# Filter diagonals from unnormalised taps, built as chunk 0 lands; transposes over three PSUM tiles; first group evacuated first

## The chip, the core and the metric

The kernel runs on one core of a Trainium2 chip. The metric is device time in microseconds of one execution, the median over several executions. The engines of the core are named as the profile names them: PE (matrix multiply; PEld is its weight loading), DVE (VectorE), ACT (ScalarE), POOL (GpSimd), and SP, which here only issues DMAs.

## What is computed

Two stages, the second fed by the first. `x` has 8 batches of 4096 tokens of 192 channels, in float32.

```python
w = exp(weight - max(weight)); w = w / sum(w)        # 8 heads x 7 taps
out[b, s, h, g] = sum_k w[h, k] * x_pad[b, s + k, h, g]   # causal, 6 zeros in front
h = out.reshape(32768, 192) @ w_in                   # 192 -> 2048
g = h * sigmoid(beta * h)                            # beta: one number per hidden column
y = g @ w_out                                        # 2048 -> 192
```

The first stage is a softmax over seven taps and a causal convolution along the tokens, the same for the 24 channels of a head. The kernel computes `silu(beta * h) @ (w_out / beta)`, which is the same as `g @ w_out`.

## The kernel before

**Tiling.** A chunk is 512 tokens of two batches, `b` and `b + 4`. The 192 channels are held as three groups of 64, and the two batches lie in the two halves of the 128 partitions, so a group is a tile of 128 partitions by 512 tokens. There are 32 chunks. For each, channels must lie on partitions, so `x` is cast to bf16 and transposed; the convolution gives `ct` (three groups); 16 hidden columns of 128 (index `u` or `fc`) are computed by `hidden`: six matmuls of 64 rows each, the two batches in the two halves of the array, then a Silu on ACT into `g`; and `Job` objects multiply `g` with `w_out_s` into the tiles `pa` and `pb`, some pairs of matmuls after each hidden column.

**Later chunks** are transposed by DMA and convolved on DVE (`tap`, L338 and L340). Their work is put between the hidden columns of the chunks before.

**Chunk 0** cannot wait for that. Its tokens land in two DMAs of 256 tokens; four blocks of 128 tokens are cast on DVE (`cast_rows`, L226) into `x0b`, transposed on PE (`transposes`, L233) and evacuated into `xt0` (L302), by ACT for blocks 0, 1 and 3 and by DVE for block 2. Groups 0 and 1 are then convolved on PE: `diag_tap` (L287) multiplies the shifted tokens with a diagonal matrix per tap, and seven of them add up in PSUM; ACT evacuates the sums (L330). Of group 2, taps 5 and 6 go this way and taps 0 to 4 run on DVE (L338, L340), and L352 adds the two.

**The taps.** `weight` is spread over the partitions by a small matmul (L244); DVE takes the maximum (L249), ACT the exponential and its sum `total` (L250), DVE the reciprocal (L252) and the product `cw` (L253), the normalised taps. `diags(k0, k1)` (L260) makes the diagonal matrices of taps `k0` to `k1 - 1` out of `cw`: taps 0 and 1 after the second cast, the others after block 2's evacuation.

**Chunk 1** is transposed on PE too (`second`); group 0 is convolved with the same diagonals in `conv1`, between hidden columns 4 to 6 of chunk 0, and evacuated by DVE (`conv1_evac`, L403); groups 1 and 2 are convolved on DVE by `conv_ops`, taken from `queue`.

**Weights.** The first 256 columns of `w_in` come by SP's queue in float32 and are cast by ACT (L332). The other columns come by eight DMAs that POOL issues (L211) and that cast on the way; two DMAs for each piece of columns, rows 0 to 63 and 64 to 127. In front of them stands a copy of one number (`hold`, L274) that makes POOL wait for `cw`. `w_out` comes by SP in four pieces and is divided by `beta` in `scale_w_out` (L314), pieces 0 and 1 on POOL and 2 and 3 on DVE. `beta` itself is transposed on PE (L308) and copied by ACT (L309); its reciprocal is L354.

**Order.** The schedule is written out by hand: each engine runs its instructions in the order in which the code emits them, and the framework adds the semaphore waits. `first_work` lists what is emitted after which hidden column of chunk 0; `None` there means the next entry of `queue`. `fill` (L223) emits matmuls of zeros between the early steps. PSUM is held in three pools: `psum_h` with two tiles and `psum_a` and `psum_b` with one each, every tile two banks large.

Of the kernel before, what the change touches and what calls it, by code (L numbers as in the profile page):

```python
# [9 lines left out]
FP32 = mybir.dt.float32  # L10
FP32R = mybir.dt.float32r
BF16 = mybir.dt.bfloat16
AF = mybir.ActivationFunctionType
ALU = mybir.AluOpType
# [3 lines left out]
def kernel(  # L18
# [17 lines left out]
    nc = tc.nc  # L36

    B, S, D = x.shape
    H, K = weight.shape
# [3 lines left out]
    NG = D // DG  # L43
    HP = group // NG
    TOK = 512
    NF = F // 128
    PAD = K - 1
    HALO = 16
    BLK = 128
# [12 lines left out]
    setup = ctx.enter_context(tc.tile_pool(name="setup", bufs=1))  # L62
# [18 lines left out]
    def in_a():  # L81
        return psum_a.tile([128, 2, TOK], FP32, name="pa")

    def in_b():
        return psum_b.tile([128, 2, TOK], FP32, name="pb")
# [85 lines left out]
    for i in range(NW - 1):  # L171
# [10 lines left out]
    xt0 = setup.tile([128, NG, HALO + TOK], FP32R)  # L182
# [6 lines left out]
        out=sel,  # L189
# [8 lines left out]
        out=sel,  # L198
# [10 lines left out]
    def load_w_in(c0, c1):  # L209
        for r in range(2):  # L210
            nc.gpsimd.dma_start(  # L211
                out=w_in_s[r * DG : (r + 1) * DG, :, c0:c1], in_=w_in_v[:, :, c0:c1]
            )
# [6 lines left out]
    def fill(n, cols=TOK):  # L220
        zc = zeros.unsqueeze(1).to_broadcast((128, cols // 128, 128))
        for _ in range(n):
            nc.tensor.matmul(pf[:, 0, 0:cols], zeros, zc, start=True, stop=True)  # L223

    def cast_rows(copy, xb, x, b):
        copy(  # L226
            xb[:, b].rearrange("q c h p -> q h c p"),
            x[:, b // 2, :, b % 2].rearrange("q h (p c) -> q h c p", c=NG),
        )

    def transposes(pt, xb, b):
        for c in range(NG):
            nc.tensor.transpose(  # L233
                pt[:, c, :], xb[:, b, c].rearrange("q h p -> q (h p)"), ident_b
            )

    def tokens(xt, b):
        t = HALO + (b // 2) * 2 * BLK
        return xt[:, :, t : t + 2 * BLK].rearrange("p c (q b) -> p c b q", b=2)[:, :, b % 2]


    fill(3)
    pw = in_a()[:, 0, 0:K]
    nc.tensor.matmul(pw, sel.rearrange("i h p -> i (h p)"), w8, start=True, stop=True)  # L244
    fill(5)
    nmax = setup.tile([128, 1], FP32)
    total = setup.tile([128, 1], FP32)
    cw = consts.tile([128, K], FP32)
    nc.vector.reduce_max(nmax, pw, axis=mybir.AxisListType.X, negate=True)  # L249
    nc.scalar.activation(cw, pw, AF.Exp, bias=nmax, accum_out=total)  # L250
    nc.scalar.activation(warm, warm, AF.Silu)
    nc.vector.reciprocal(total, total)  # L252
    nc.vector.tensor_scalar_mul(cw, cw, total)  # L253

    beta = consts.tile([128, NF], FP32)
    beta_r = setup.tile([128, NF], FP32)
    diag = setup.tile([128, K, 128], FP32R)

    def diags(k0, k1):
        nc.vector.tensor_tensor(  # L260
            diag[:, k0:k1],
            ident.unsqueeze(1).to_broadcast((128, k1 - k0, 128)),
            cw[:, k0:k1].unsqueeze(2).to_broadcast((128, k1 - k0, 128)),
            ALU.mult,
        )

    for b in range(NB):
        cast_rows(nc.vector.tensor_copy, x0b, x0, b)
        if b == 1:
            diags(0, 2)  # L270


    hold = setup.tile([1, 1], FP32)
    nc.gpsimd.tensor_copy(hold, cw[0:1, 0:1])  # L274
    load_w_in(F0, FW)
    for i in range(1, NW):
        load_w_in(i * FW, (i + 1) * FW)
# [2 lines left out]
    cts = {}  # L280
# [4 lines left out]
    def diag_tap(k, xt, pv, rows=slice(0, 128), k0=0):  # L285
        o = HALO - PAD + k
        nc.tensor.matmul(  # L287
            pv,
            diag[rows, k, :],
            xt[rows, o : o + TOK],  # L290
            start=(k == k0),
            stop=(k == K - 1),
        )

    pts = [
        pool.tile([128, 2, 2 * TOK], BF16, name=name)
        for pool, name in ((psum_b, "pb"), (psum_h, "ph"))
    ]
    for b in range(NB):
        pt = pts[b % 2][:, b // 2, 0 : NG * BLK].rearrange("p (c q) -> p c q", c=NG)  # L300
        transposes(pt, x0b, b)
        (nc.vector.tensor_copy if b == 2 else nc.scalar.copy)(tokens(xt0, b), pt)  # L302
        if b % 2:
            fill(1, 384 if b > 1 else 128)
    diags(2, 4)
    diags(4, K)
    pb = in_a()[:, 0, 0:NF]
    nc.tensor.transpose(pb, beta_q, ident[0:NF, 0:NF])  # L308
    nc.scalar.copy(beta, pb)  # L309
    fill(1, 128)  # L310

    def scale_w_out(i):
        fcs = slice(i * NQ, (i + 1) * NQ)
        (nc.vector if i > 1 else nc.gpsimd).tensor_tensor(  # L314
            w_out_s[:, fcs, :],
            w_out_raw[:, fcs, :],
            beta_r[:, fcs].unsqueeze(2).to_broadcast((128, NQ, D)),
            ALU.mult,
        )
# [3 lines left out]
    for c in range(NG - 1):  # L323
        pv = in_b() if c else psum_h.tile([128, 2, TOK], FP32, name="ph")
        for k in range(K):
            diag_tap(k, xt0[:, c], pv[:, 0, :])
        if c == 0:
            for b in range(2):
                cast_rows(nc.scalar.copy, x1b, x1, b)
        nc.scalar.copy(cts[0][:, c, :], pv[:, 0, :])  # L330
        if c == 0:
            nc.scalar.copy(w_in_s[:, :, 0:F0], w_in_raw)  # L332
    cast_rows(nc.scalar.copy, x1b, x1, 2)

    def tap(dst, src, k):
        scalar = cw[:, k : k + 1]
        if k == 0:
            nc.vector.tensor_scalar_mul(dst, src, scalar)  # L338
        else:
            nc.vector.scalar_tensor_tensor(  # L340
                out=dst, in0=src, scalar=scalar, in1=dst, op0=ALU.mult, op1=ALU.add
            )

    K_V = 5
    pv = in_a()[:, 0, :]
    for k in range(K_V, K):
        diag_tap(k, xt0[:, NG - 1], pv, k0=K_V)
    dst = cts[0][:, NG - 1, :]
    for k in range(K_V):
        o = HALO - PAD + k  # L350
        tap(dst, xt0[:, NG - 1, o : o + TOK].bitcast(FP32), k)
    nc.vector.tensor_tensor(dst, pv, dst, ALU.add)  # L352
    cast_rows(nc.vector.tensor_copy, x1b, x1, 3)
    nc.vector.reciprocal(beta_r, beta)  # L354
    scale_w_out(0)
    scale_w_out(1)


    def second():
# [39 lines left out]
    def conv1_evac():  # L399
        pv = conv1_ps[0]  # L400
        for r in range(2):
            rows = slice(r * DG, (r + 1) * DG)
            nc.vector.tensor_copy(cts[1][rows, 0, :], pv[rows, r, :])  # L403

    def conv_ops(s, c0):
        def op(k):
# [115 lines left out]
    def rows_of(ch):  # L522
# [3 lines left out]


    first_work = {
        4: [None, None],
        5: [None],  # L530
        6: [conv1_evac, lambda: scale_w_out(2), None],
        7: [None, lambda: rows_of(2)],
        8: [lambda: scale_w_out(3), None],
# [75 lines left out]
```

## Time and profile before

| what | value |
|---|---|
| median of 4 runs | 690.13 us (690.09 to 690.46) |
| profiled execution: its time | 690.46 us |
| profiled execution: its span | 688.7 us |
| PE busy | 683.1 us, 99% |
| ACT busy | 578.8 us, 84% |
| DVE busy | 524.6 us, 76% |
| POOL busy | 10.8 us, 2% |
| granted clock of PE | 1.000 |

The span runs from the first to the last instruction; the execution's own time is 1.8 us more. Times in the profile are microseconds from the start of the span. A row of the profile names the engine, the line of the kernel, the operation and the tiles as `out<-in`, then shapes as partitions by elements, a count, and in brackets the idle time before it and what ended that. The chain of waits is followed back from the last instruction: at each step to what released it, or to the instruction before it on its engine. Instructions of one engine are pipelined, so that one can start up to about 0.1 us before the end of the one before it.

### The profile page before, as it was taken

What the parts mean: (1) busy time and instruction counts of PE and PEld (TensorE: products, weight loads), DVE (VectorE), ACT (ScalarE), POOL (GpSimd) and SP (SyncE); (2) the same over time, 40 slices, a digit from 0 to 9 for tenths busy, and PEclk for the clock granted to TensorE, in tenths of its full rate; (3) what the DMA queues carried; (4) which work ended last, traced back from release to release, by engine and by line L of the source; (5) the groups of instructions that cost most, each with busy time, mean ns of one, the idle gap of its engine ahead of it and who ended that gap; (6) DMA issues with size and microseconds to landing.
All of it is one profiled execution on the core that took longest, in us unless ns stands there. A gap on an engine that the chain in (4) does not pass through costs nothing.

```text
span 688.7 us, 24344 instructions
## 1 busy us (share of the span) xinstructions
PE 683.1 (99%) x11312; PEld 522.2 (76%) x11312; DVE 524.6 (76%) x467; ACT 578.8 (84%) x530; POOL 10.8 (2%) x20
## 2 busy tenths in 40 slices
PE   8999999999999999999999999999999999999998
PEld 4777777777777777777777777777777777777777
DVE  7889877788777797777797777887777977777712
ACT  7988888888888888888888888888888888888893
POOL 5100000000000000000000000000000000000000
PEclk9999999999999999999999999999999999999999
DMA  9744333244332343332344432443323433322111
GB/s 228 188 104 117 105 100 88 60 116 116 93 106 69 85 116 108 101 100 55 104 117 105 93 88 66 116 117 93 105 54 99 117 106 98 97 62 59 49 36 59
DMA packets 121861, 67.06 MB, mean 97 GB/s; under 512 B 53264, under 2 KB 121760, under 8 KB 121760
## 3 DMA queue, kind: packets, MB, share of 16 engines
q1 hardware_dynamic: 120048, 64.12, 34.7%
q0 software_dynamic: 1664, 1.38, 1.2%
q8 instruction: 88, 1.44, 1.0%
q14 instruction: 13, 0.11, 0.1%
q10 hardware_dynamic: 48, 0.01, 0.0%
HBM read 29.89 MB, written 25.17 MB: 80 GB/s over the span
## 4 chain that ended last, share of the span: by engine, by line
PE 98%; DVE 1%; ACT 0%; issue 0%; DVEq 0%; ACTq 0%
PE ph L424 48%; PE pa L457 25%; PE pb L457 24%; PE ph L223 1%; DVE ct L340 0%; PE pb L287 0%; ACT g L432 0%; PE pb L233 0%; DVE ct L352 0%; DVE diag L260 0%; DVE xt L302 0%; PE pa L244 0%; ACT xt L302 0%; DVE ct L338 0%; ACT osb L473 0%
## 5 line engine op out<-in xcount | busy, mean ns | idle before, releaser
L432 ACT ACTIVATE g<-ph,beta 128x1024 bf16<-128x1024 f32 x512 | 569.7, 1115 | 94.9 <-PE ph L424 90.2
L457 PEld LDWEIGHTS <-g 64*128 64x128 bf16 x8160 | 371.0, 94 | 102.2 <-issue 0.2
L424 PE MATMUL ph<-ct,w_in_s 64*128 64x512 bf16 x3072 | 425.2, 376 | 1.0 <-ACT g L432 0.9
L340 DVE SCALAR_TENSOR_TENSOR ct<-xt,cw,ct 128x1536 bf16<-128x1536 bf16 (+2 forms) x190 | 338.0, 1779 | 2.5
L457 PE MATMUL pa<-w_out_s,g 64*128 64x192 bf16 x4112 | 245.3, 243 | 0.0
L457 PE MATMUL pb<-w_out_s,g 64*128 64x192 bf16 (+1 forms) x4048 | 230.4, 243 | 0.0
L424 PEld LDWEIGHTS <-w_in_s 64*128 64x128 bf16 x3072 | 160.0, 94 | 54.7 <-DMA w_in_s<-in_moe_w_in_dram 1.1
L475 DVE TENSOR_REDUCE osb<-pa 128x384 f32<-128x768 f32 x64 | 61.3, 958 | 122.5 <-PE pa L457 121.4
L475 DVE TENSOR_REDUCE osb<-pb 128x384 f32<-128x768 f32 x63 | 60.3, 958 | 29.0 <-PE pb L457 29.0
L106 DVE CAST xb<-xf 128x768 bf16<-128x768 f32 x60 | 40.5, 677 | 0.0
L338 DVE TENSOR_SCALAR ct<-xt,cw 128x1536 bf16<-128x1536 bf16 (+2 forms) x32 | 31.2, 976 | 0.0
L473 ACT COPY osb<-pb 128x192 f32<-128x192 f32 x1 | 0.3, 319 | 7.2 <-PE pb L457 7.2
L223 PE MATMUL ph<-zeros 128*128 128x512 bf16 (+2 forms) x11 | 4.6, 535 | 1.1 <-DVE warm L180 1.1
L211 POOL DMA_DIRECT2D w_in_s<-in_moe_w_in_dram x8 | 5.3, 672 | 0.0
L287 PE MATMUL pb<-xt,diag 64*128 64x512 f32 (+1 forms) x21 | 5.2, 443 | 0.0
L121 DVE COPY xt<-xt 128x18 bf16<-128x18 bf16 x27 | 4.4, 163 | 0.0
L314 POOL TENSOR_TENSOR w_out_s<-w_out_raw,beta_r 128x768 bf16<-128x768 f32 x2 | 3.9, 1964 | 5.4 <-DVE beta_r L354 3.5
L287 PEld LDWEIGHTS pb<-xt,diag 64*128 64x128 f32 (+1 forms) x21 | 3.2, 187 | 1.1 <-issue 0.4
L223 PEld LDWEIGHTS <-zeros 128*128 128x128 bf16 x11 | 1.2, 126 | 2.2 <-issue 1.1
L181 ACT ACT_TABLE_LOAD x1 | 1.3, 1283 | 1.8 <-issue 1.8
L226 ACT CAST x1b<-x 128x384 bf16<-128x384 f32 x3 | 2.0, 718 | 0.0
L233 PEld LDWEIGHTS <-x0b 128*128 128x128 bf16 x12 | 1.2, 129 | 1.0 <-issue 0.5
(55 smaller groups left out, 28.5 us busy)
## 6 DMA issues: line engine op xcount, KB each, us to landing
out_dram<-osb SPq DMA_DIRECT2D x127, 192.0 KB, 2.2
xf<-in_x_dram SPq DMA_DIRECT2D x60, 384.0 KB, 4.4
xt<-xb SPq DMA_TRANSPOSE x120, 2.8
x<-in_x_dram SPq DMA_DIRECT2D x4, 384.0 KB, 4.8
w_out_raw<-in_moe_w_out_dram SPq DMA_DIRECT2D x4, 384.0 KB, 12.7
w_in_s<-in_moe_w_in_dram POOLq DMA_DIRECT2D x6, 192.0 KB, 11.5
w_in_raw<-in_moe_w_in_dram SPq DMA_DIRECT2D x2, 192.0 KB, 6.8
w_in_s<-in_moe_w_in_dram POOLq DMA_DIRECT2D x2, 96.0 KB, 8.4
```

The costliest lines, as they stand in the source:

```text
L106: nc.vector.tensor_copy(xbs[ch][:, :, :, h, :], xfs[ch][:, h].rearrange("q b (p c) -> q b c p", c=NG),)
L121: nc.vector.tensor_copy(dst, last[:, :, HALO + TOK - PAD :])
L211: nc.gpsimd.dma_start(out=w_in_s[r * DG : (r + 1) * DG, :, c0:c1], in_=w_in_v[:, :, c0:c1])
L223: nc.tensor.matmul(pf[:, 0, 0:cols], zeros, zc, start=True, stop=True)
L287: nc.tensor.matmul(pv, diag[rows, k, :], xt[rows, o : o + TOK], start=(k == k0), stop=(k == K - 1),)
L314: (nc.vector if i > 1 else nc.gpsimd).tensor_tensor(w_out_s[:, fcs, :], w_out_raw[:, fcs, :], beta_r[:, fcs].unsqueeze(2).to_broadcast((12 ...
L338: nc.vector.tensor_scalar_mul(dst, src, scalar)
L340: nc.vector.scalar_tensor_tensor(out=dst, in0=src, scalar=scalar, in1=dst, op0=ALU.mult, op1=ALU.add)
L424: nc.tensor.matmul(ph[:, h, :], w_in_s[rows, j, fc * 128 : (fc + 1) * 128], cts[s][rows, j, :], start=(j == 0), stop=(j == NG - 1),)
L432: nc.scalar.activation(gs[s][:, fc], ph, AF.Silu, scale=beta[:, fc : fc + 1])
L457: nc.tensor.matmul(self.po[:, r, b * D : (b + 1) * D], g[rows, fc, self.h, q * BLK : (q + 1) * BLK], w_out_s[rows, fc, :], start=(self.don ...
L475: nc.vector.tensor_reduce(dst, self.po[:, :, 0 : nb * D].rearrange("p r n -> p n r"), axis=mybir.AxisListType.X, op=ALU.add,)
```

## The change

The diagonals are made from `eu`, the exponentials before division by their sum, and the division is applied where the sums leave PSUM, by a factor `rn` per partition: ACT's two evacuations multiply by `rn`, the last sum of group 2 becomes a multiply and add, and chunk 1's evacuation multiplies too. `rn` and `cw` (still used by the taps on DVE) are made after block 2's evacuation.

Taps 0 to 3 of the diagonals are now built before the first cast, the other three after the second cast; POOL's `hold` reads the diagonals and so waits for the first four.

The four transposed blocks go to three tiles in place of two: block 2 to the second bank of the tile that held the taps' product, block 3 to the second bank of `pb`. Blocks 2 and 3 are evacuated in two instructions each, group 0 first and groups 1 and 2 after it. The transposed `beta` goes to a free bank of the second `ph` tile. Piece 1 of `w_out` is scaled on DVE, emitted after hidden column 4 and between the first and the second tap of chunk 1.

```diff
-    pw = in_a()[:, 0, 0:K]
+    pc = in_a()
+    pw = pc[:, 0, 0:K]
...
+    rn = setup.tile([128, 1], FP32)
     cw = consts.tile([128, K], FP32)
+    eu = setup.tile([128, K], FP32)
     nc.vector.reduce_max(nmax, pw, axis=mybir.AxisListType.X, negate=True)
-    nc.scalar.activation(cw, pw, AF.Exp, bias=nmax, accum_out=total)
+    nc.scalar.activation(eu, pw, AF.Exp, bias=nmax, accum_out=total)
     nc.scalar.activation(warm, warm, AF.Silu)
-    nc.vector.reciprocal(total, total)
-    nc.vector.tensor_scalar_mul(cw, cw, total)
...
-            cw[:, k0:k1].unsqueeze(2).to_broadcast((128, k1 - k0, 128)),
+            eu[:, k0:k1].unsqueeze(2).to_broadcast((128, k1 - k0, 128)),
...
+    diags(0, 4)
     for b in range(NB):
         cast_rows(nc.vector.tensor_copy, x0b, x0, b)
         if b == 1:
-            diags(0, 2)
+            diags(4, K)
...
-    nc.gpsimd.tensor_copy(hold, cw[0:1, 0:1])
+    nc.gpsimd.tensor_copy(hold, diag[0:1, 0, 0:1].bitcast(FP32))
...
+    banks = [pts[0][:, 0], pts[1][:, 0], pc[:, 1].bitcast(BF16), pts[0][:, 1]]
     for b in range(NB):
-        pt = pts[b % 2][:, b // 2, 0 : NG * BLK].rearrange("p (c q) -> p c q", c=NG)
+        pt = banks[b][:, 0 : NG * BLK].rearrange("p (c q) -> p c q", c=NG)
         transposes(pt, x0b, b)
-        (nc.vector.tensor_copy if b == 2 else nc.scalar.copy)(tokens(xt0, b), pt)
+        copy = nc.vector.tensor_copy if b == 2 else nc.scalar.copy
+        for cs in (slice(0, 1), slice(1, NG)) if b > 1 else (slice(0, NG),):
+            copy(tokens(xt0, b)[:, cs], pt[:, cs])
         if b % 2:
             fill(1, 384 if b > 1 else 128)
-    diags(2, 4)
-    diags(4, K)
-    pb = in_a()[:, 0, 0:NF]
+    pb = pts[1][:, 1, 0 : 2 * NF].bitcast(FP32)
     nc.tensor.transpose(pb, beta_q, ident[0:NF, 0:NF])
     nc.scalar.copy(beta, pb)
     fill(1, 128)
+    nc.vector.reciprocal(rn, total)
+    nc.vector.tensor_scalar_mul(cw, eu, rn)
 
     def scale_w_out(i):
-        (nc.vector if i > 1 else nc.gpsimd).tensor_tensor(
+        (nc.vector if i else nc.gpsimd).tensor_tensor(
...
-        nc.scalar.copy(cts[0][:, c, :], pv[:, 0, :])
+        nc.scalar.mul(cts[0][:, c, :], pv[:, 0, :], rn)
...
-    nc.vector.tensor_tensor(dst, pv, dst, ALU.add)
+    nc.vector.scalar_tensor_tensor(
+        out=dst, in0=pv, scalar=rn, in1=dst, op0=ALU.mult, op1=ALU.add
+    )
...
-    scale_w_out(1)
...
-            nc.vector.tensor_copy(cts[1][rows, 0, :], pv[rows, r, :])
+            nc.vector.tensor_scalar_mul(cts[1][rows, 0, :], pv[rows, r, :], rn[rows])
...
     first_work = {
-        4: [None, None],
+        4: [None, lambda: scale_w_out(1), None],
```

## The prediction

> **What bounds the kernel now.** I read the page first, for the engine that is never free; then the chain of waits in the first 17 us, where all the edits lie; then the order of time around 16 us, and the DMA queues, for what ends the waits there.
>
> The page, parts 1 and 4 (busy time by engine; the chain that ended last):
>
> ```profile
> PE 683.1 (99%) x11312; PEld 522.2 (76%) x11312; DVE 524.6 (76%) x467; ACT 578.8 (84%) x530; POOL 10.8 (2%) x20
> ...
> PE 98%; DVE 1%; ACT 0%; issue 0%; DVEq 0%; ACTq 0%
> ```
>
> PE is the bound once chunk 0 runs. A start-up edit can only move the moment from which PE is dense, so I ask what sets that. The chain of waits, us 7 to 17:
>
> ```profile
> 7.59 0.55 DVE diag L260
> 8.14 0.47 DVE ct L338
> 8.63 0.77 DVE ct L340
> ...
> 11.85 0.70 DVE ct L352
> 12.55 0.04 issue
> 12.60 0.41 PE ph L424 x2
> ...
> 13.09 2.13 ACT g L432 x2
> 15.21 0.04 issue
> 15.26 0.82 PE ph L424 x6
> 16.08 0.47 PE pb L287 x2
> 16.55 0.57 PE ph L424 x2
> ```
>
> Up to 12.55 the chain is VectorE: the diagonals, then the five taps and the sum of chunk 0's third group. But the step at 16.55 hides a wait, because one half of the array was busy. In order of time, us 16 to 19:
>
> ```profile
> 16.36 0.09 PEld L424 LDWEIGHTS <-w_in_s 64*128 64x128 bf16 x1
> 16.37 1.19 PE L424 MATMUL ph<-ct,w_in_s 64*128 64x512 bf16 x6
> 16.49 2.46 POOL L314 TENSOR_TENSOR w_out_s<-w_out_raw,beta_r 128x768 bf16<-128x768 f32 x1 [1.91 <-DMA w_out_raw<-in_moe_w_out_dram]
> 16.73 0.33 PEld L424 LDWEIGHTS <-w_in_s 64*128 64x128 bf16 x5 [0.28 <-DMA w_in_s<-in_moe_w_in_dram]
> ```
>
> This is hidden column 4 of chunk 0. The weights of rows 0 to 63 are there and load at 16.36; those of rows 64 to 127 (the fourth DMA that POOL issues) are not, and load at 16.73, the moment they land (16.69 by issue 6.51 plus 10.2 to landing, rounded). From there PE has no gap above 0.15 us. So the landing of a weight DMA, and not the VectorE chain, starts the dense stretch. What starts that DMA, POOL in order of time:
>
> ```profile
> 4.17 0.17 POOL L274 COPY hold<-cw 1x1 f32<-1x1 f32 x1 [1.94 <-DVE cw L253]
> 4.29 5.32 POOL L211 DMA_DIRECT2D w_in_s<-in_moe_w_in_dram  x8
> ```
>
> POOL issues the eight weight DMAs behind a copy that waits for `cw`. Last the queues, first us 9 to 10, then 10 to 17; before 9 the view has no packet of q0 at all:
>
> ```profile
> q0 software_dynamic: 27, 0.01, 10.0%
> ...
> q0 software_dynamic: 1082, 0.85, 75.1%
> q1 hardware_dynamic: 1086, 0.82, 45.5%
> ```
>
> The weights' queue q0 starts past 9 and then shares full engines with q1 until about 20.
>
> **The change part by part.** The sum is against the profiled execution (span 688.7, its time 690.46, 0.33 above the median 690.13); the difference is carried to the median.
>
> *Diagonals from `eu`, early.* VectorE loses the reciprocal and multiply at 3.67 to 4.10 and builds four diagonals there. Rows by form: 256 elements 421 ns, 384 elements 554 ns, so 133 ns per 128, and 512 elements about 687 ns: 3.67 to 4.36. Chunk 0's first rows land at 4.30 and the casts start at 4.32; instructions overlap by 0.09, so the first cast is at most 0.04 late. The other three diagonals (554 ns for 427) push casts 2 and 3 from 5.35 to about 5.44. In return 0.89 us of diagonals leaves the chain at 7.25.
>
> *The POOL hold.* It now waits for the first diagonals: 4.36 for 4.10, so hold and all eight weight issues move by **+0.26**. Behind it on POOL stand those DMAs and the first `w_out` scaling, which waits for 12.7 anyway. How much of 0.26 reaches the landing is unknown: nothing if q0's start near 9.4 is set by something else, all of it if set by the issue. From 10 to 17 both queues stay loaded, so a late q0 has no idle engine to catch up on; I take 0.26 and keep 0. An earlier landing is not excluded: VectorE's work beside the issues changes, and the first issue took 913 ns against 627, so I allow −0.29.
>
> The Trainium skill speaks against the whole shift: "DMA: Bandwidth & Descriptors", section "Latency and other measured facts", puts the first byte of a software-generated DMA about 1 us after its issue. The first issue ends at 5.20 and q0's first packets come after 9, so the trace does not agree. If the page were right, something other than the issue would hold q0 back and could absorb the shift: the sum would be 690.13 by the page, 690.39 by the rows.
>
> *Transposes in three tiles, split evacuations.* Block 2 no longer waits for ScalarE's evacuation (6.15): its transposes start near 6.0 for 6.20, and VectorE's copy at 6.55 for 6.78. The 559 ns copy becomes 128 + 256 elements, at 133 ns per 128 about 293 + 426 less 0.09 overlap: 0.63, done 7.18. ScalarE's block 3 likewise ends near 7.35 for 7.47. One more instruction costs 0.07 to 0.16 (smallest rows 98 to 164 ns) on each engine, inside these figures. The convolution matmuls start on the first group, at about 7.1 for 7.52; they are not the chain, VectorE is.
>
> *Reciprocal and `cw` moved here.* 164 + 230 ns and a 35 ns gap, after the copy: 7.09 to 7.52; with the 0.105 gap of a two-semaphore wait the first tap starts at 7.62 for 8.05. Taps unchanged (3.69 to the end of the last): 11.31.
>
> *`rn` in the evacuations.* The sum at L352 (692 ns) becomes a scalar_tensor_tensor; 752 ns is that operation's row: 11.42 to 12.17 for 12.54, **−0.37**. ScalarE's two evacuations cost 583 as CAST; by ACTIVATE rows (1114 ns for 1024, 202 for one element) up to 658. The first has 0.7 us of idle time beside it, the second ends by 11.75, before the 12.17 that PE needs. VectorE's two at L403 (683, 695) cost at most 752: +0.13, against 0.29 of slack (last tap of chunk 1 ends 30.05, PE needs it at 30.38).
>
> *`w_out` scaling 1 from POOL to VectorE.* 0.96 us (the L314 row on VectorE), behind a wait for a DMA that lands at 16.43. Queued behind it: two taps of chunk 1, then the evacuation at 20.50, which waits for PE 0.47. The second of those taps took 2.37 us for 1.28 while POOL scaled; I take 1.28 back. So 16.47, 17.43, 18.7, 20.0: still before 20.50. Off the path; if that cover is gone it costs 1 us per us.
>
> *`beta`'s transpose* goes to a free half of another tile; nothing waits for it before 12.
>
> *Sum.* The 0.37 travels to column 0 (12.22 for 12.60). Column 2 meets its own late weights: 13.71 + 0.26 gives 14.02 for 14.25, so 0.23 is left. Column 4's first half starts near 16.04 for 16.37, and then its second half waits for 16.69 + 0.26 = 16.95, starting 16.99 for 16.73. The gain ends in that wait, and the shift remains: **+0.26 us, 690.39**.
>
> **The rivals.**
> *The issue does not set the landing (0): 690.13.* For: q0 starts 4 us after the first issue. Against: the DMA engines were not full between 6 and 8 us (84.5% busy, 181 GB/s against 328 after 9), so a q0 that was ready would have been served there.
> *Weights are no gate: faster.* The median is 0.33 below the profiled run, about the 0.37 between the two halves of column 4; perhaps in other executions the weights land earlier and PE sets 16.37. Then 16.04 for 16.37: −0.33, 689.80. It decides if the weights land 0.65 us or more earlier than in this profile.
> *VectorE waits for `w_out`: slower.* The scaling sits ahead of chunk 1's taps. It has 20.50 + 0.26 − 20.0 = 0.77, and 0.29 at chunk 1's start: 1.06 in all. It decides if that DMA lands after 17.5. It took 11.6 us to land; with the slowest of its line, 13.7, it costs 2.1 − 1.06 = 1.04 more: 691.43. Against: it is ahead of q0 in time, and q0 starts later now.
> *The change does not do what it says:* the order of instructions shows that it does; only its worth is open.
>
> **How the numbers follow.** Forecast 0.58, no shift 0.17, faster 0.17, `w_out` 0.05, anything else 0.03. The predicted time is the forecast's, 690.39; its own range is 690.20 to 690.60 (a shift of 0.26 give or take 0.2, since runs of one kernel differ by 0.37 here). The range of 8 in 10 takes in the shift of nothing, the earlier landing (690.13 − 0.29 = 689.84) and the faster rival with 0.15 beyond it, and above 0.2 of a late `w_out`: 689.65 to 690.80. All three main cases lie within 0.2% (1.38 us, about what a measurement of this kernel can tell from no change): same 0.90, slower 0.07 (`w_out` later still, or a start-up that I misread), faster 0.03.
>
> **What would show it.** Hold at about 4.43; first tap at 7.6; the sum of group 3 ending near 12.2; column 4's second weight load near 17.0 with a longer wait for the weight DMA behind its name (about 0.8 us); scaling 1 on VectorE from 16.5 after a wait for `w_out_raw`, and the tap after it at 1.28 us. Wrong if that weight load stays at 16.7 or comes before, or if PE waits anywhere between 17 and 31.

## The result and the profile after

The changed kernel takes **691.42 us** (median of 32 executions, 690.34 to 692.05) against 690.21 us for the kernel before beside it (52 executions): a ratio of 1.0013, 95% interval 1.0008 to 1.0018. The forecast was 690.39 us, with a range that ended at 690.80. By the ratio the kernel is slower by about 0.9 us (the two medians differ by 1.21), which is more than the measurement is uncertain and less than the 0.2% that the chances were counted by.

The page of the changed kernel, parts 1, 3 and 4 (busy time by engine; one DMA queue; the chain that ended last):

```profile
PE 682.4 (99%) x11312; PEld 535.6 (78%) x11312; DVE 524.5 (76%) x468; ACT 579.3 (84%) x531; POOL 8.4 (1%) x19
...
q14 instruction: 14, 0.11, 0.1%
...
PE 97%; DMA 1%; POOL 0%; ACT 0%; ACTq 0%; DVE 0%; issue 0%
```

PE is still the bound and is no busier than before. The chain now has a DMA in it. The chain of waits of the changed kernel, us 5 to 22, shows which:

```profile
4.74 2.14 POOL w_in_s L211 x3
6.88 9.77 DMA w_in_s<-in_moe_w_in_dram
16.65 0.05 issue
16.69 0.69 PE ph L431 x5
```

The VectorE chain is gone from it. POOL's issues and the landing of column 4's weights are what PE waits for, as the prediction said, but they land at 16.65, not at 16.95. In order of time, PE's weight loads of the changed kernel show the wait itself:

```profile
15.68 0.09 PEld L431 LDWEIGHTS <-w_in_s 64*128 64x128 bf16 x1
16.69 0.33 PEld L431 LDWEIGHTS <-w_in_s 64*128 64x128 bf16 x5 [0.92 <-DMA w_in_s<-in_moe_w_in_dram]
```

The wait grew from 0.28 to 0.92 us, and the load starts at 16.69 for 16.73. From here on the two traces are one: column 4's Silu starts 0.05 us earlier than before, the activations of chunk 1 within 0.00, ACT's last copy at 685.44 in both. So the start-up costs nothing in these two executions, and **all of the 0.98 us by which the spans differ lies behind 685.8 us**, in a stretch that the prediction never looked at. What SP waits for there (us in total, times, longest), in the kernel before:

```profile
SPq L604 <- DMA out_dram<-osb: 1.2, 1, 1.2
```

and in the changed kernel:

```profile
SPq L611 <- DMA out_dram<-osb: 2.2, 1, 2.2
```

The last output is issued at 685.79 in both and is 1.0 us later to land in the second. The DMA view of 686.3 to 687.1 us (queue: packets, MB, share of the DMA engines) shows that output in the kernel before:

```profile
q1 hardware_dynamic: 144, 0.10, 37.2%
```

and in the changed kernel:

```profile
q1 hardware_dynamic: 135, 0.09, 35.7%
```

The next stretch, 687.1 to 688.2 us, has nothing in the kernel before:

```profile
DMA packets 0, 0.00 MB, mean 0 GB/s; under 512 B 0, under 2 KB 0, under 8 KB 0
```

and in the changed kernel:

```profile
q1 hardware_dynamic: 9, 0.01, 2.3%
q14 instruction: 1, 0.01, 1.7%
```

One packet of 8 KB on q14, a queue of instructions, starts at 687.24 and takes 307 ns; as it ends, nine packets of the last output follow, from 687.55 to 687.91. In the kernel before, all 144 packets of that output have moved by 687.1; here 135 have, and these nine come late. Nine is a sixteenth of 144, so they look like the share of one DMA engine that was held up by the instructions; the trace does not name the engine of a packet, so that last step is arithmetic.

**Whose instructions.** Most q14 packets stand at the same times in both traces, within 0.4 us. Three do not: 220.31, 534.13 and 689.56 before, 199.82, 513.66 and 687.24 after. The change makes ACT's instruction stream 579 long for 577 (semaphore instructions counted; the trace itself has 578 and 576 records of ACT, one less in every kernel): one more copy for block 3 and one more semaphore instruction before ACT's first evacuation of the sums (L336). PE's instruction queue, q8, moved 88 packets of 16 KB for 22,635 instructions, 257 each; so an instruction is about 64 bytes, and 8 KB are 128.

A refill is the fetch of the next such block. ACT's packets (in the kernel before 53.20, 220.31, 367.02, 534.13 and 689.56) fit refills that are asked for when its sequencer, the part that reads its instructions, comes to index 64, 192, 320, 448 and 576, the records of these numbers in the trace. By the times, the sequencer runs ahead of the engine as far as the next wait: in the changed kernel record 192 ran at 218.0, and the packet came at 199.82, 1.4 us after the last semaphore in front of that record (198.40). In all ten profiles of this document, each of these five packets starts 1.0 to 1.7 us after the last semaphore instruction or drain (DRAIN in the trace; the one at the end of the kernel ends 0.04 us behind the last copy) in front of its index; with the index moved by one record either way, some are off by 2 to 22 us. In the changed kernel index 576 is a semaphore instruction right behind a drain that ends at 685.80, while the last output is on its way; before, it is the last instruction of the stream, reached at 688.25, and the refill falls after the end.

### The profile page after: what moved, and what is told of

Read it like the earlier page. It is cut to its first block, busy times and chain, and to the rows that moved or that the text cites. A ratio compares the mean times of both kernels' runs of the same rounds, so it can differ in the third digit from the quotient of the medians.

```text
span 689.7 us, 24346 instructions
## 1 busy us (share of the span) xinstructions
PE 682.4 (99%) x11312; PEld 535.6 (78%) x11312; DVE 524.5 (76%) x468; ACT 579.3 (84%) x531; POOL 8.4 (1%) x19
## 4 chain that ended last, share of the span: by engine, by line
PE 97%; DMA 1%; POOL 0%; ACT 0%; ACTq 0%; DVE 0%; issue 0%
PE ph L431 48%; PE pa L464 25%; PE pb L464 24%; DMA w_in_s<-in_moe_w_in_dram 1%; POOL w_in_s L211 0%; PE pb L289 0%; ACT L181 0%; DVE diag L261 0%; ACTq L151 0%; ACT eu L253 0%; ACTq L153 0%; ACT osb L480 0%; POOL hold L276 0%; ACT warm L181 0%
## 5 line engine op out<-in xcount | busy, mean ns | idle before, releaser
L464 PEld LDWEIGHTS <-g 64*128 64x128 bf16 x8160 | 380.3, 94 | 92.8 <-issue 0.2
L431 PE MATMUL ph<-ct,w_in_s 64*128 64x512 bf16 x3072 | 429.9, 376 | 1.4 <-ACT g L439 0.7
L464 PE MATMUL pa<-w_out_s,g 64*128 64x192 bf16 x4112 | 249.2, 243 | 0.0
L464 PE MATMUL pb<-w_out_s,g 64*128 64x192 bf16 (+1 forms) x4048 | 233.6, 243 | 0.0
L431 PEld LDWEIGHTS <-w_in_s 64*128 64x128 bf16 x3072 | 169.2, 94 | 50.7 <-DMA w_in_s<-in_moe_w_in_dram 1.8
L320 DVE TENSOR_TENSOR w_out_s<-w_out_raw,beta_r 128x768 bf16<-128x768 f32 x3 | 2.9, 952 | 0.0
L410 DVE TENSOR_SCALAR ct<-pb,rn 64x512 bf16<-64x512 f32 x2 | 1.5, 750 | 1.5 <-PE pb L289 1.5
```

The costliest lines, as they stand in the source:

```text
L320: (nc.vector if i else nc.gpsimd).tensor_tensor(w_out_s[:, fcs, :], w_out_raw[:, fcs, :], beta_r[:, fcs].unsqueeze(2).to_broadcast((128, N ...
L431: nc.tensor.matmul(ph[:, h, :], w_in_s[rows, j, fc * 128 : (fc + 1) * 128], cts[s][rows, j, :], start=(j == 0), stop=(j == NG - 1),)
L464: nc.tensor.matmul(self.po[:, r, b * D : (b + 1) * D], g[rows, fc, self.h, q * BLK : (q + 1) * BLK], w_out_s[rows, fc, :], start=(self.don ...
```

## The experiments

The first theory is this refill: what counts is how many instructions ACT has, not what they do. Its rival is that the change's start-up costs the time in most executions, and that the profiled one was lucky. ACT's stream was made longer or shorter in both kernels by instructions on `warm`, a tile of one element on each of eight partitions.

**The kernel before with the changed kernel's length (579).**

```diff
     cast_rows(nc.scalar.copy, x1b, x1, 2)
+    nc.scalar.copy(warm, warm)
+    nc.scalar.copy(warm, warm)
+    nc.scalar.copy(warm, warm)
```

> The kernel before with three tiny copies of the one-element tile `warm` added on ScalarE early in chunk 0: nothing of the change, but ScalarE's instruction stream grows from 577 to 579 (one semaphore instruction falls away), the length that the changed kernel has. Theory (the refill of ScalarE's instruction stream lands on the last output transfer): a row of instruction DMA of 8 KB at about 687.2 us, SP's wait for the last output about 2.2 us for 1.2, and a median 0.7 to 1.2 us above the kernel before, about 691.2. Rival (what the change did at the start of the kernel costs the time): the start is as before, so the median is too, 690.2, within 0.2.

Measured: 691.09 us against 690.35 for the kernel before; ratio 1.0011, interval 1.0002 to 1.0021. SP's waits:

```profile
SPq L607 <- DMA out_dram<-osb: 1.9, 1, 1.9
```

The DMA view of 686.3 to 687.1 us in the same kernel:

```profile
q1 hardware_dynamic: 135, 0.09, 34.2%
q14 instruction: 1, 0.01, 5.1%
```

And of 687.1 to 688.2 us:

```profile
q1 hardware_dynamic: 9, 0.01, 1.7%
```

The refill is there, at 686.52 us for the 687.2 expected; it takes 652 ns, and again 135 packets come in time and nine late, from the moment it ends. None of the change is in this kernel, and it has most of the loss: 0.74 us between the medians for the changed kernel's 1.21, and nearly the same ratio. The rival falls as the explanation of that part.

**The kernel before with one copy more (578).**

```diff
     cast_rows(nc.scalar.copy, x1b, x1, 2)
+    nc.scalar.copy(warm, warm)
```

> The kernel before with one tiny copy of `warm` on ScalarE: 578 instructions. A control for the first of these runs: by the refill theory index 576 is still behind the last barrier, so no refill lands on the last output and the median stays 690.2 within 0.2. If any growth of ScalarE's stream costs time, in proportion, about a third to a half of what three copies cost: 690.5.

Measured: 690.20 us against 690.35; ratio 0.9997, 0.9988 to 1.0006. The refill is at 689.34, and SP waits 1.2 us. A longer stream costs nothing by itself.

**The changed kernel with one instruction less (578).**

```diff
-    nc.scalar.activation(warm, warm, AF.Exp)
```

> The changed kernel without the first activation of the one-element tile `warm` (the table load stays): ScalarE's stream is 578 instructions for 579, everything of the change stays. Theory (refill on the last output): the refill comes after the end, SP waits 1.2 us, and the median is 690.2, the kernel before's, within 0.3. Rival (the change's start-up costs the time): 691.1 to 691.4, as the changed kernel.

Measured: 690.34 us against 690.35; ratio 1.0000, 0.9991 to 1.0009. SP's waits:

```profile
SPq L610 <- DMA out_dram<-osb: 1.2, 1, 1.2
```

The DMA view of 688.5 to 690 us, after the last output:

```profile
DMA packets 1, 0.01 MB, mean 5 GB/s; under 512 B 0, under 2 KB 0, under 8 KB 0
...
q14 instruction: 1, 0.01, 2.1%
```

All of the change is in it, one tiny activation is not, and the loss is gone. So the start-up of the change costs nothing that these runs can tell, and the rival falls whole.

**The changed kernel with one instruction more (580).**

```diff
     cast_rows(nc.scalar.copy, x1b, x1, 2)
+    nc.scalar.copy(warm, warm)
```

> The changed kernel with one more tiny copy of `warm` on ScalarE: 580 instructions. Theory (refill on the last output, and its place set by which instruction has index 576): the refill is asked for at the first drain, about 684.4 us, and lands near 685 to 686, ahead of the last output's packets (from 686.4): 690.2 within 0.3, although the kernel does more work than the changed one. Rivals: the start-up costs the time, or more ScalarE instructions cost more: 691.1 to 691.6.

Measured: 690.27 us against 690.35; ratio 0.9997, 0.9988 to 1.0006. SP's waits:

```profile
SPq L612 <- DMA out_dram<-osb: 1.2, 1, 1.2
```

The DMA view of 684.5 to 686.4 us in the same kernel, its last line an issue (tiles, engine, operation, count, KB each, median us to landing):

```profile
q14 instruction: 1, 0.01, 1.9%
...
out_dram<-osb SPq DMA_DIRECT2D x2, 96.0 KB, 2.4
```

This is the sharpest of the four: the kernel does **more** than the changed one and is 1.1 us faster. The refill came at 685.37, ahead of the last output: the median landing of the two outputs that the window shows is 2.4 us, against 1.6 in the kernels with no refill there. Those outputs have time to spare, and the last one has none.

**One part undone, and the changed kernel again.** Of the change, block 3's split copy is what lengthened the stream. Here it is one copy again:

```diff
-        for cs in (slice(0, 1), slice(1, NG)) if b > 1 else (slice(0, NG),):
+        for cs in (slice(0, 1), slice(1, NG)) if b == 2 else (slice(0, NG),):
```

> The changed kernel with one part undone: ScalarE evacuates block 3 in one copy as before (VectorE's block 2 stays split, and everything else of the change stays). ScalarE's stream is 578 for 579. Theory (refill on the last output): the 8 KB of instructions come after the end, near 688.9, SP waits 1.2 us for the last output, median 690.2 to 690.4. Rival (the change costs its time in the start-up, of which the split is a hidden part): 691.1 to 691.4, as the changed kernel, or more, since the first convolution matmul starts later.

> The changed kernel once more, unaltered, beside the version with block 3 in one copy. If the refill falls where it fell before: 8 KB at about 687.2, SP waits 1.9 to 2.2 us, median 691.1 to 691.4. If its place varies from run to run, the wait and the median vary with it, down to 690.3.

Measured on one chip: block 3 whole 690.63 us, ratio 1.0004 (0.9995 to 1.0013), SP's wait 1.2 us, refill at 688.70; the changed kernel again 691.33 us, ratio 1.0011 (1.0002 to 1.0020), refill at 686.94. SP's waits of the latter:

```profile
SPq L611 <- DMA out_dram<-osb: 1.8, 1, 1.8
```

The unsplit version's median is 0.2 us above what was expected, with an interval that holds no change. The place of the refill differs by 0.3 us between the two profiles of the changed kernel, and SP's wait by 0.4.

The medians come from three sets of runs, in which the kernel before had 690.21, 690.35 and 690.15; the ratio goes by the runs of its own set.

| kernel | ACT stream | refill starts, us | SP's last wait, us | median, us | ratio to before |
|---|---|---|---|---|---|
| before | 577 | 689.56 | 1.2 | 690.21 | |
| before, one copy more | 578 | 689.34 | 1.2 | 690.20 | 0.9997 |
| changed, one activation less | 578 | 688.93 | 1.2 | 690.34 | 1.0000 |
| changed, block 3 whole | 578 | 688.70 | 1.2 | 690.63 | 1.0004 |
| **before, three copies more** | **579** | **686.52** | **1.9** | **691.09** | **1.0011** |
| **changed** | **579** | **687.24** | **2.2** | **691.42** | **1.0013** |
| **changed again** | **579** | **686.94** | **1.8** | **691.33** | **1.0011** |
| changed, one copy more | 580 | 685.37 | 1.2 | 690.27 | 0.9997 |

**Does the issue of the weights set the dense stretch?** This was the term that the forecast rested on. With the tail clean (578), `hold` was moved both ways.

```diff
-    nc.gpsimd.tensor_copy(hold, diag[0:1, 0, 0:1].bitcast(FP32))
+    nc.gpsimd.tensor_copy(hold, eu[0:1, 0:1])
```

> The 578-instruction version of the changed kernel (median 690.34, no refill on the last output) with `hold` reading `eu` instead of the first diagonal, so POOL issues the weight loads about 0.75 us earlier (first one near 3.9 for 4.68). If the issue sets the landing one to one and column 4's second-half weights are the gate of the dense stretch (the prediction's theory): landing near 15.8 for 16.43, PE's wait for them (0.72 us) nearly gone, median 0.4 to 0.7 below, 689.6 to 689.9. Rival (issue does not set the landing, since x and w_out hold the DMA engines until 9 us): landing stays 16.4 within 0.2, median 690.3. Second rival (landing moves, but the next weights or chunk 1 take the gain back): landing 15.8, median 690.2 to 690.4.

```diff
-    nc.gpsimd.tensor_copy(hold, diag[0:1, 0, 0:1].bitcast(FP32))
+    nc.gpsimd.tensor_copy(hold, x0b[0:1, 2, 0, 0, 0:1])
```

> The same 578-instruction version with `hold` reading the cast third block of x, ready near 5.82, so the weight loads are issued about 1.4 us later (first one near 6.1 for 4.68). If issue sets landing one to one and that landing is the gate: column 4's second-half weights at 17.8 for 16.43, PE waits 2.1 us for 0.72, median 1.2 to 1.5 above 690.34, 691.6 to 691.8. Rival (issue does not set landing): landing 16.4 within 0.3, median 690.3. In between (a slope of a half): landing 17.1, median 691.0.

Measured: early 690.05 us (ratio 0.9998, 0.9989 to 1.0007), late 691.04 us (1.0009, 1.0000 to 1.0018), against 690.27 for the kernel before. The early one issued its first weight DMA at 4.35, not 3.9, since the copy on POOL took 0.70 us; its median missed the 689.6 to 689.9 that were expected. Its weights land at 15.88, and PE does not wait for them at all. PE's weight loads there:

```profile
15.98 0.35 PEld L430 LDWEIGHTS <-w_in_s 64*128 64x128 bf16 x6
```

The chain of waits of the late one:

```profile
5.93 0.31 POOL hold L275
6.24 2.07 POOL w_in_s L210 x3
8.31 8.64 DMA w_in_s<-in_moe_w_in_dram
16.95 0.05 issue
17.00 0.69 PE ph L430 x5
```

The fourth weight DMA is issued 1.43 us later than in the changed kernel with 578 (8.31 for 6.88) and lands 0.52 later (16.95 for 16.43). So here the landing moved by a third of the issue and not one to one, and the cost arrives at the end: the span is 0.50 longer, the median 0.70. The size of that share is not settled: a straight line through the ten profiles below gives 0.42 us of landing per us of issue, with a standard error of 0.18. Of the nine other profiles, seven have column 4 shifted against the kernel before by just what its weights' landing is shifted, within 0.02 us:

| kernel | fourth weight DMA issued | landed | column 4's Silu against before |
|---|---|---|---|
| before | 6.51 | 16.69 | 0 |
| changed | 6.88 | 16.65 | -0.05 |
| changed again | 6.94 | 16.80 | +0.11 |
| before, 579 | 6.48 | 16.39 | -0.30 |
| before, 578 | 6.45 | 15.91 | +0.17 (VectorE late) |
| changed, 578 | 6.88 | 16.43 | -0.26 |
| changed, block 3 whole | 6.89 | 16.21 | -0.48 |
| changed, 580 | 7.00 | 16.55 | -0.15 |
| weights early | 6.55 | 15.88 | -0.73 (no wait) |
| weights late | 8.31 | 16.95 | +0.26 |

In every profile ACT's last copy, at the end of 32 chunks, has that same shift within 0.05 us: what is won or lost at column 4 stays to the end. But landings with the same issue scatter by 0.6 to 0.8 us (15.88 to 16.69 for issues at 6.45 to 6.55, mean 16.22; 16.21 to 16.80 for 6.88 to 7.00, mean 16.53).

Weights early has the lowest median of all, 1.3 to 1.4 us below the changed kernel, and 1.1 of that is the missing instruction (690.34); against the kernel before its interval holds no change, so it beats that one by nothing that can be told.

## Why the prediction was wrong

**The step that failed** is half a sentence under the split evacuations: "One more instruction costs 0.07 to 0.16 ... on each engine, inside these figures". It priced an instruction by its duration, where it stands. One more ACT instruction and the semaphore instruction beside it cost nothing there; they moved the refill by two instructions, into the last output, 680 us later, where SP's wait for that output grew by 0.6 to 1.0 us in the three profiles with 579. With it fell the sentence "A start-up edit can only move the moment from which PE is dense": the tail after the last matmul was taken as fixed. None of the rivals held it either. What could have warned was there before: q14's packet at 689.56 in the trace, less than three us behind the last packets of an output that the whole program waits for, and a change that alters the length of a stream.

**PE bound, column 4's weights the gate:** right in eight of ten profiles, and the two in which the weights are not the gate are those with the earliest landings.

**POOL's hold:** right in place (4.43, as forecast), too small in size. The fourth issue moved by 0.37 for 0.26, because the hold copy itself took 0.31 us for 0.17.

**Landing +0.26:** mis-sized, and not readable from one profile. It measured -0.04 in the profiled pair. Over the two groups of issues above it is +0.31 for 0.42 of issue (16.53 for 16.22), with a scatter twice that; the late version gives 0.52 for 1.43. The rival "the issue does not set the landing" is made unlikely by this, not excluded, and its price, 0, was nearer to the profiled pair. What the issue plainly moves is the start of q0: its first packet came at 9.32, 9.43, 9.88, 9.92, 10.17 and 10.88 us for first issues at 4.35, 4.29, 4.69, 4.68, 4.80 and 6.19, and in all ten profiles 4.7 to 5.4 us behind the issue.

**VectorE chain -0.37:** measured -0.68 in the changed kernel, -0.33 to -0.70 over the versions of it. The operations cost what was forecast (diagonals 694 ns for 687, the last sum 750 for 752). What differed is PE, whose transposes were done sooner, so that VectorE's copy began at 6.25 for the 6.55 forecast: the interval between matmuls of 512 columns fell from 427 to 217 ns at about 4.4 us, where in the kernel before the transposes of 128 columns still had 107 ns at 6.3 and 55 from 6.6. It fell at 5.3 in the changed kernel run again and at 5.5 in the kernel before with 578, and only after 6.4 with block 3 whole and in both versions that move the weights; so the moment varies between executions, while the granted clock that the profile prints is 1.00 from the first microsecond. The Trainium skill, "TensorE: Matmul & The Clock Gate", Part 1, has such a halving and says that the window which decides it runs free, so that the same kernel warms up at different moments; the intervals agree, the printed clock does not show it. In the three versions of the change where it fell only after 6.4, as in the kernel before, the chain moved by -0.33 to -0.39: the forecast's -0.37 was right for that pace of PE, and the rest of the -0.68 is luck.

**Where the gain ends:** right. Whatever VectorE won was eaten at column 4, as the wait of 0.92 for 0.28 shows. One more wait for weights came behind it, 0.2 us on PE's weight loads at column 8 (landing at 21.32 for 19.75); it was made up before chunk 1, whose activations stand where they stood.

**Evacuations with `rn`:** ScalarE's cost 687 and 689 ns, above the bound of 658; VectorE's 742 and 757, at the bound of 752. Both hidden, as said. (The slack of 0.29 behind the latter is 0.33 by the prediction's own times, 30.05 and 30.38.)

**Scaling 1 on VectorE:** cheaper than forecast. VectorE in order of time, changed kernel:

```profile
15.54 0.95 DVE L320 TENSOR_TENSOR w_out_s<-w_out_raw,beta_r 128x768 bf16<-128x768 f32 x1
16.41 2.60 DVE L346 SCALAR_TENSOR_TENSOR ct<-xt,cw,ct 128x1024 bf16<-128x1024 bf16 x2
```

There is no wait: this `w_out` piece had landed at 14.09, for the 16.43 of the kernel before. Both taps behind it take 1.28 us, and the 2.37 us that one took beside POOL's scaling is gone. In all ten profiles it lands between 13.10 and 16.43, never after the 17.5 that the rival "VectorE waits for `w_out`" needed.

**The faster rival** (690.13 less 0.33) had its mechanism right: with the weights early, column 4 started 0.73 us sooner and the span was 0.59 shorter. That version's median is 0.2 below the kernel before, inside the scatter. Its price of 0.33 (16.04 for 16.37) does not follow from the prediction's sum, which leaves 0.23 after column 2, or the whole 0.37 where column 2's weights come earlier too; the forecast does not use it.

## What to carry to other kernels

Before a sum is closed, count each engine's instructions before and after an edit, and look where its instruction packets fall against the last output; the end of a kernel is a critical path of its own. When a kernel loses a microsecond that no stage shows, add and remove one instruction that does nothing, in the old and in the new version: if the time jumps back, the loss is a place in the stream and not the edit. A term smaller than the scatter of a landing between executions (here 0.6 to 0.8 us) can't be settled by one pair of profiles.

## What the runs showed of the hardware

- An engine's instructions come by DMA, and their packets can hold up packets of data. In three profiles an 8 KB packet of 307 to 652 ns stood in front of the last nine packets of the output, which started within 0.01 us of its end, and SP waited 1.8 to 2.2 us for 1.2. Why 307 ns of packet cost 1.0 us of wait is open: in the changed kernel no packet of the output moves from 687.06 to 687.55, although the instruction packet starts only at 687.24.
- The Trainium skill, "Runtime: NRT & Kernel Launch", section "Instruction fetch mechanics", says that each engine refills its instruction memory in 16 KiB blocks over its own DMA queue while it executes. For PE the trace agrees: 88 packets of 16 KB on a queue of their own, 257 instructions each. For ACT it does not: the packets that move with its stream have 8 KB.
- The last refill starts 1.0 to 1.4 us after ACT's sequencer can reach index 576, in all ten profiles. Two expectations rested on that index and held: 578 is free, 580 is free. That 64 + 128 n is the rule of the sequencer is inferred from this kernel and its variants alone.
